# Three PSUM banks taken through one pool of three buffers, or through three names strictly in turn

## The chip, the cores and the metric

One NeuronCore of a Trainium2 chip runs the kernel. The metric is device time in microseconds (us), the median of the timed executions; in the profiles it is the span of one execution. Differences are judged from executions of both kernels on one chip, in the same rounds. Engines are named PE or TensorE (matmul), PEld (its weight loads), DVE or VectorE, ACT or ScalarE, POOL or GpSimd, SP or SyncE.

## The reference

A recurrent retention layer (4 sequences, 8 heads, 768 steps, head size 64) feeds a two-layer network with a SiLU between (3072 tokens, 512 to 2048 to 512), all in fp32:

```python
for t in range(S):                               # attention, by head with decay gamma
    state = gamma * state + einsum('bhd,bhe->bhde', k[:, :, t], v[:, :, t])
    y[:, :, t] = scale * einsum('bhd,bhde->bhe', q[:, :, t], state)
x = y.transpose(0, 2, 1, 3).reshape(B * S, H * D)
h = x @ w_in
out = (h * (1 / (1 + exp(-h)))) @ w_out
```

## The kernel before

The sequence is cut into 6 chunks of 128 steps. A *visit* handles one chunk of one sequence: TensorE transposes k and q (tiles kp and qp), forms scores and state sums, then the outputs y. A *product* is 1/16 of the first layer for one chunk: 8 matmuls into the accumulator ha and 4 into hb (three fp32 products of split operands, for accuracy). Visits are woven in between products. The results g go to memory and come back for the last stage, the second layer.

PSUM has eight banks here: two for the scores (s), two for y, one for qp (q), and three that kp, ha and hb share, through one name with three buffers. The framework picks a bank from those that are free when it lays out the program, and adds a semaphore wait to the first matmul of a tile for whoever used that bank last.

```python
ps_u = pool("ps_u", 1, space=PS)
ps_h = pool("ps_h", 3, space=PS)
...
def turn(name):
    return ps_h.tile([128, 512], FP32, tag="h", name=name)
...                                                  # in a visit
for name, to, bufs, src, tp in (
        ("kt", kt, 2, kqv["k"][n], turn(f"kp_{n}")),
        ("qt", qt, 3, kqv["q"].pop(n), banks("q", f"qp_{n}", 1)[:, 0])):
    ...                                              # 4 transposes by TensorE into tp
    evac[:] = [nc.scalar.copy(out=to[n], in_=tp).ins]          # ScalarE empties kp, qp
...
def product_in(c, f):
    ha, hb = turn(f"ha_{c}_{f}"), turn(f"hb_{c}_{f}")
    for i in range(3):
        for kk in range(KIN):
            nc.tensor.matmul(hb if i == 2 else ha, ...)
    hs = hpool.tile([128, NT], FP32, tag="hs", name=f"g_{c}_{f}")
    nc.scalar.activation(out=hs, in_=ha, func=AF.Copy, scale=ONE_E)        # empties ha
    nc.vector.tensor_tensor(out=hs, in0=hs, in1=hb, op=ALU.subtract)       # empties hb
    nc.scalar.activation(out=hs, in_=hs, func=AF.Silu)
...                                                  # last stage: accumulators of 4 sequences
acc.append([turn(f"oa{b}_{c}"), turn(f"ob{b}_{c}") if b == 2 else
            banks("q", f"ob{b}_{c}", 1)[:, 0]])
...
nc.scalar.dma_start(out=out[...], in_=o)             # outputs leave by ScalarE's queue
```

TensorE's order is the program's own; the framework orders the other engines.

Of the kernel before, what the change touches and what calls it, by code (L numbers as in the profile page):

```python
# [12 lines left out]
FP32 = mybir.dt.float32  # L13
# [18 lines left out]
def kernel(  # L32
# [42 lines left out]
    PS = bass.MemoryType.PSUM  # L75

    def pool(name, bufs, **kw):
        return ctx.enter_context(tc.tile_pool(name=name, bufs=bufs, **kw))
# [8 lines left out]
    stage = pool("stage", 2)  # L87
    conv = pool("conv", 1)
    ps_u = pool("ps_u", 1, space=PS)
    ps_h = pool("ps_h", 3, space=PS)  # L90

    g_dram = {(c, f): dram.tile([128, NT], FP32, tag=f"g{c}_{f}", name=f"gd_{c}_{f}")
              for c in range(NC) for f in range(NF)}
# [186 lines left out]
    def banks(tag, name, n=2):  # L280
        return ps_u.tile([128, n, 512], FP32, tag=tag, name=name)

    def turn(name):
        return ps_h.tile([128, 512], FP32, tag="h", name=name)

    token = const.tile([1, 1], FP32, tag="token", name="token")

# [22 lines left out]
    def stage_t(n):  # L310
# [4 lines that stand above are left out]
            tp = tp.rearrange("p (a t) -> p a t", a=HP)  # L315
            for a in range(HP):
                nc.tensor.transpose(tp[:, a, :], src[:, 2 * a : 2 * a + 2, :], ident)
            to[n] = one.tile([128, HP, C], FP32, tag=name, name=f"{name}_{n}", bufs=bufs)
            evac[:] = [nc.scalar.copy(out=to[n], in_=tp).ins]
# [148 lines left out]
# [4 lines that stand above are left out]
                nc.tensor.matmul(hb if i == 2 else ha, lhsT=w_sb[f][:, i, ts(kk, 128)],  # L472
                                 rhs=xt[c][:, i, kk, :], start=kk == 0 and i != 1,
                                 stop=kk == KIN - 1 and i != 0)
        hs = hpool.tile([128, NT], FP32, tag="hs", name=f"g_{c}_{f}")
        nc.scalar.activation(out=hs, in_=ha, func=AF.Copy, scale=ONE_E)  # L476
        nc.vector.tensor_tensor(out=hs, in0=hs, in1=hb, op=ALU.subtract)  # L477
        nc.scalar.activation(out=hs, in_=hs, func=AF.Silu)  # L478
        pending.append((c, f, hs))
# [95 lines left out]
    for c in range(NC):  # L575
        acc = []
        for b in range(B):
            if b < 2:
                u = banks("sy"[b], f"o{b}_{c}")
                acc.append([u[:, i] for i in range(2)])  # L580
            else:
                acc.append([turn(f"oa{b}_{c}"), turn(f"ob{b}_{c}") if b == 2 else
                            banks("q", f"ob{b}_{c}", 1)[:, 0]])
        for f in range(NF):
            n = c * NF + f
            split(n + S_AHEAD)
            t = ready.pop(n)
            first_, last = f == 0, f == NF - 1
            for b in range(B):
                gh, glo, gm = (t[:, i, ts(b, C)] for i in range(3))  # L590
                oa, ob = acc[b]
                nc.tensor.matmul(oa, lhsT=gh, rhs=wo[f][:, 0, :], start=first_, stop=False)  # L592
                nc.tensor.matmul(oa, lhsT=glo, rhs=wo[f][:, 1, :], start=False, stop=last)  # L593
                nc.tensor.matmul(ob, lhsT=gm, rhs=wo[f][:, 2, :], start=first_, stop=last)  # L594
        for b in range(B):
            oa, ob = acc[b]
            o = one.tile([128, DM], FP32, tag=("kt", "qt")[b % 2], name=f"o_{c}_{b}",
                         bufs=(2, 3)[b % 2])
            nc.scalar.activation(out=o, in_=oa, func=AF.Copy, scale=ONE_E)
            nc.vector.tensor_tensor(out=o, in0=o, in1=ob, op=ALU.subtract)  # L600
            nc.scalar.dma_start(out=out[ds(b * S + c * C, C), :], in_=o)
# [30 lines left out]
```

## Time and profile before

| | before |
|---|---|
| time, median of 3 executions | 658.88 us (657.73 to 659.81) |
| span of the profiled execution | 659.4 us |
| TensorE busy | 619.9 us, 94% |
| idle of TensorE up to 92 us | 24.5 us |
| waits of TensorE for one of the three banks, by the list of waits | 6.2 us |

The profile lines are shown in the prediction: busy times first, then the stretches, then TensorE's waits.

### The profile page before, as it was taken

The numbers are of one execution on the slowest core, as the hardware profiler recorded it, in microseconds if no ns is written. First come the engines' busy times: TensorE is split into PE (matmuls) and PEld (weight loads), VectorE is DVE, ScalarE is ACT, GpSimd is POOL, SyncE is SP. The second block draws the span as 40 slices with busy tenths as digits, with TensorE's granted clock in tenths as the row PEclk, the third lists the DMA queues.
The fourth block names the chain that finished last, engine by engine and source line by source line (L and its number), as shares of the span: only waits on it lengthen the run. The fifth ranks groups of instructions, "written<-read, shape, count | busy, mean of one in ns | idle before, by whom it ended". The sixth has DMA issues, their size and how long they took to land.

```text
span 659.4 us, 13529 instructions
## 1 busy us (share of the span) xinstructions
PE 619.9 (94%) x5440; PEld 507.2 (77%) x5440; DVE 429.2 (65%) x740; ACT 282.0 (43%) x510; POOL 14.2 (2%) x94
## 2 busy tenths in 40 slices
PE   3679898999999989999999999999999999999996
PEld 2557786778778877888878888888888888888885
DVE  4988887989666886775948757454463545554631
ACT  5435555757544445444548863222131412222311
POOL 2000100000000000000000000000000000000000
PEclk9869999999999999999999999999999999999999
DMA  9967777555656776766646645342343432423301
GB/s 204 205 153 172 194 185 198 171 175 187 213 153 183 207 223 181 225 178 223 196 157 198 195 147 163 89 167 93 100 156 100 133 123 95 160 95 97 129 0 64
DMA packets 123070, 103.64 MB, mean 157 GB/s; under 512 B 80000, under 2 KB 88192, under 8 KB 123008
## 3 DMA queue, kind: packets, MB, share of 16 engines
q1 hardware_dynamic: 119552, 96.49, 50.7%
q10 hardware_dynamic: 3456, 6.29, 2.6%
q8 instruction: 42, 0.69, 0.4%
q14 instruction: 20, 0.16, 0.1%
HBM read 66.06 MB, written 36.70 MB: 156 GB/s over the span
## 4 chain that ended last, share of the span: by engine, by line
PE 66%; DVE 16%; DMA 6%; ACT 5%; issue 3%; SPq 2%; POOL 0%; ACTq 0%; DVEq 0%; POOLq 0%
PE ha L472 15%; PE hb L472 8%; PE ob L594 7%; PE o L594 7%; PE o L592 7%; PE oa L592 7%; PE o L593 7%; PE oa L593 7%; DMA wf<-in_moe_w_in_dram 3%; DVE g L477 2%; DVE cs L189 2%; DVE cp L193 2%; PE y L375 2%; DVE xt L417 1%; ACT ca L182 1%
## 5 line engine op out<-in xcount | busy, mean ns | idle before, releaser
L472 PE MATMUL ha<-xt,wi 128*128 128x512 f32 x768 | 197.3, 398 | 9.9 <-DVE g L477 4.3
L472 PEld LDWEIGHTS ha<-xt,wi 128*128 128x128 f32 x768 | 142.2, 189 | 47.0 <-DVE g L477 9.0
L519 DVE TENSOR_TENSOR gs<-gr,gs 128x512 fp32r<-128x512 f32 x96 | 62.2, 686 | 89.5 <-ACT gs L517 89.5
L517 ACT ACTIVATE gs<-gr 128x512 fp32r<-128x512 f32 x96 | 53.6, 621 | 134.1 <-issue 131.8
L472 PE MATMUL hb<-xt,wi 128*128 128x512 f32 x384 | 104.4, 394 | 0.5 <-ACT g L476 0.2
L477 DVE TENSOR_TENSOR g<-g,hb 128x512 f32<-128x512 f32 x96 | 65.7, 684 | 50.4 <-PE hb L472 39.6
L478 ACT ACTIVATE g<-g 128x512 f32<-128x512 f32 x96 | 60.6, 631 | 77.0 <-DVE g L477 76.2
L472 PEld LDWEIGHTS hb<-xt,wi 128*128 128x128 f32 x384 | 72.1, 189 | 18.1 <-ACT g L476 1.5
L594 PE MATMUL ob<-wo,gs 128*128 128x512 f32 x192 | 75.2, 392 | 0.0
L592 PE MATMUL o<-wo,gs 128*128 128x512 f32 x192 | 74.7, 389 | 0.0
L592 PE MATMUL oa<-wo,gs 128*128 128x512 f32 x192 | 74.7, 389 | 0.0
L594 PE MATMUL o<-wo,gs 128*128 128x512 f32 x192 | 74.7, 389 | 0.0
L593 PE MATMUL o<-wo,gs 128*128 128x512 f32 x192 | 74.7, 389 | 0.0
L593 PE MATMUL oa<-wo,gs 128*128 128x512 f32 x192 | 74.7, 389 | 0.0
L476 ACT ACTIVATE g<-ha 128x512 f32<-128x512 f32 x96 | 56.4, 588 | 28.7 <-PE ha L472 25.6
L520 DVE SCALAR_TENSOR_TENSOR gs<-gs 128x512 fp32r<-128x512 f32 x96 | 62.0, 685 | 0.0
L594 PEld LDWEIGHTS ob<-wo,gs 128*128 128x128 f32 x192 | 36.0, 188 | 8.9 <-DVE o L600 1.6
L593 PEld LDWEIGHTS o<-wo,gs 128*128 128x128 f32 x192 | 36.0, 188 | 7.6
L594 PEld LDWEIGHTS o<-wo,gs 128*128 128x128 f32 x192 | 36.0, 188 | 7.5
L592 PEld LDWEIGHTS oa<-wo,gs 128*128 128x128 f32 x192 | 36.0, 188 | 7.5
L593 PEld LDWEIGHTS oa<-wo,gs 128*128 128x128 f32 x192 | 36.0, 188 | 7.5
L592 PEld LDWEIGHTS o<-wo,gs 128*128 128x128 f32 x192 | 36.0, 188 | 7.3
(71 smaller groups left out, 639.9 us busy)
## 6 DMA issues: line engine op xcount, KB each, us to landing
gd<-g SPq DMA_DIRECT2D x96, 256.0 KB, 3.0
gr<-gd SPq DMA_DIRECT2D x96, 256.0 KB, 2.7
wf<-in_moe_w_out_dram SPq DMA_DIRECT2D x16, 512.0 KB, 4.3
kf<-in_k_dram SPq DMA_DIRECT2D x24, 256.0 KB, 4.9
qf<-in_q_dram SPq DMA_DIRECT2D x24, 256.0 KB, 4.5
vf<-in_v_dram SPq DMA_DIRECT2D x24, 256.0 KB, 4.9
out_dram<-o ACTq DMA_DIRECT2D x24, 256.0 KB, 2.1
wf<-in_moe_w_in_dram SPq DMA_DIRECT2D x16, 256.0 KB, 3.4
```

Of the source, the lines that this page charges most:

```text
L189: nc.vector.scalar_tensor_tensor(out=s, in0=a, scalar=3, in1=s, op0=ALU.logical_shift_left, op1=ALU.bitwise_or)
L193: nc.vector.scalar_tensor_tensor(out=p.bitcast(FP32), in0=lo, scalar=2.0 ** -52, in1=p.bitcast(FP32), op0=ALU.mult, op1=ALU.mult)
L472: nc.tensor.matmul(hb if i == 2 else ha, lhsT=w_sb[f][:, i, ts(kk, 128)], rhs=xt[c][:, i, kk, :], start=kk == 0 and i != 1, stop=kk == KIN ...
L476: nc.scalar.activation(out=hs, in_=ha, func=AF.Copy, scale=ONE_E)
L477: nc.vector.tensor_tensor(out=hs, in0=hs, in1=hb, op=ALU.subtract)
L478: nc.scalar.activation(out=hs, in_=hs, func=AF.Silu)
L517: nc.scalar.activation(out=t[:, 0, :], in_=g, func=AF.Copy, scale=HALF)
L519: nc.vector.tensor_tensor(out=t[:, 1, :], in0=g, in1=high, op=ALU.subtract)
L520: nc.vector.scalar_tensor_tensor(out=t[:, 2, :], in0=t[:, 1, :].bitcast(FP32), scalar=-1.0 / EPS, in1=high, op0=ALU.mult, op1=ALU.add)
L592: nc.tensor.matmul(oa, lhsT=gh, rhs=wo[f][:, 0, :], start=first_, stop=False)
L593: nc.tensor.matmul(oa, lhsT=glo, rhs=wo[f][:, 1, :], start=False, stop=last)
L594: nc.tensor.matmul(ob, lhsT=gm, rhs=wo[f][:, 2, :], start=first_, stop=last)
```

## The change

Its intent is to take the three banks strictly in turn, each under a name of its own, rather than as the layout happens to find them free.

```diff
-    ps_h = pool("ps_h", 3, space=PS)
+    ps_h = pool("ps_h", 1, space=PS)
...
+    turns = [0]
+
     def turn(name):
-        return ps_h.tile([128, 512], FP32, tag="h", name=name)
+        turns[0] += 1
+        return ps_h.tile([128, 512], FP32, tag=f"h{turns[0] % 3}", name=name)
```

## The prediction

> **What bounds the kernel now.** I read the page first (busy times and the strip of 40 slices), then the busy times by stage, then TensorE's list of waits, and last the timeline around the place where, as will be seen, the change acts.
>
> ```profile
> PE 619.9 (94%) x5440; PEld 507.2 (77%) x5440; DVE 429.2 (65%) x740; ACT 282.0 (43%) x510; POOL 14.2 (2%) x94
> ...
> PE   3679898999999989999999999999999999999996
> ...
> PEclk9869999999999999999999999999999999999999
> ```
>
> The first line is busy time by engine, the second TensorE's share of each of 40 slices in tenths, the third its granted clock. TensorE is the bound: 619.9 of 659.4 us, and only the first three slices, of 16.5 us each, are below 8 tenths.
>
> ```profile
> core 0: us, PE busy (x) PEld busy (x) DVE busy (x) ACT busy (x) POOL busy (x), PEclk, DMA share, GB/s
> 0.00:92.00 92.00, 67.53 (x1408) 55.43 (x1408) 72.77 (x135) 45.38 (x93) 8.48 (x62) 0.91 0.81 185
> 92.00:192.00 100.00, 95.15 (x718) 75.51 (x711) 80.56 (x142) 60.22 (x105) 1.49 (x6) 1.00 0.60 185
> 192.00:391.00 199.00, 194.13 (x2172) 159.85 (x2171) 141.78 (x246) 106.68 (x188) 4.21 (x26) 1.00 0.65 194
> 391.00:659.40 268.40, 263.13 (x1157) 216.41 (x1155) 134.10 (x217) 69.72 (x126) 0.00 (x0) 1.00 0.34 110
> ```
>
> This is busy time by stretch. From 92 us on TensorE is busy 95.15 of 100, 194.13 of 199 and 263.13 of 268.40 us. The only stretch with room is the first, with 92 - 67.53 = 24.5 us idle, and it is also where attention fills the state and the first products start. What TensorE waits for:
>
> ```profile
> PE kp L317 <- DMA kf<-in_k_dram: 10.3, 2, 7.0
> PE y L375 <- DVE xt L417: 8.5, 4, 3.3
> PE ha L472 <- DVE g L477: 4.3, 9, 1.6
> PE ha L472 <- DVE xt L417: 3.4, 3, 1.4
> PE kp L317 <- DVE g L477: 1.7, 3, 1.4
> ...
> PE hb L472 <- ACT g L476: 0.2, 1, 0.2
> ```
>
> The columns are total us, times, longest us. The three banks that the change is about hold kp (k's transposes), ha and hb (the two halves of a product). A wait for one of these banks can only show as a wait for whoever empties it: ScalarE's copy of kp (line 319), ScalarE's reading of ha (line 476), VectorE's subtraction that reads hb (line 477). Such rows sum to 4.3 + 1.7 + 0.2 = 6.2 us, 0.94% of the span. That is a ceiling: even a perfect handling of these banks could not give 2% (13.2 us). The larger rows wait for an input's transfer or for the split of x, which the change doesn't touch.
>
> **What the Trainium skill says.** "Perfetto Trace Analysis", section "Matmuls", says independent groups of matmuls should rotate through different PSUM banks, so that emptying one overlaps the matmuls of the next. The kernel before does so already, and the trace agrees: at 63.37 us TensorE writes the next ha while ScalarE reads the last one from 63.87 and VectorE the last hb from 65.68. "PSUM — Partial Sum Buffer", section "The four PSUM rules", says that each bank is a separate SRAM and one matmul targets a single bank. Nothing there makes one bank slower than another. The trace shows no difference either: all 768 matmuls into ha have a median of 389 ns and all 384 into hb too, over all three banks. "Perfetto Trace Analysis", section "Identifying Dependency Chains", says to look at the semaphores that an instruction waits for. That settles this case, since a bank's name costs nothing by itself: only a different wait can.
>
> **The change part by part.** It removes no instruction and adds none. It replaces one pool name with three buffers by three names with one buffer each, the name chosen by a counter. So it can act in only two ways: another order of instructions, or another bank, and with it another wait, for some tile. I built both kernels and compared them. The order on all five engines is the same, row for row. TensorE's order is fixed by the program anyway.
>
> Of the tiles that go through the turn (24 kp, 192 ha and hb, and 18 accumulators of the last stage, three for each of six chunks) eight get another bank. With the three banks called 5, 6, 7:
>
> ```
> tile:    kp0 kp1 kp2 kp3 kp4 kp5 ha0 hb0 kp6 ha1 hb1 kp7 ha2 hb2 ha3 hb3 kp8
> before:   5   7   6   5   7   6   5   7   6   5   7   6   5   6   7   5   6
> after:    5   6   7   5   6   7   5   6   7   5   6   7   5   6   7   5   6
> ```
>
> (ha0 is the first product of chunk 0, and so on.) The pool of three was therefore already taken in turn everywhere, but with 6 and 7 exchanged at first; at hb2 the two swapped once, and from there on before and after are the same bank for bank to the end. While the labels are merely exchanged, each tile follows the same predecessor in its bank, so its wait is the same. Only the two tiles at the swap have another predecessor, and the built programs differ in exactly two waits, both on TensorE: hb2 waited for ScalarE's copy of kp7, and will wait for VectorE's subtraction that reads hb1; ha3 has it the other way round. All other semaphore waits, over all engines, have the same semaphore and value.
>
> Are these two on the path? The timeline of before, TensorE, then VectorE, then ScalarE:
>
> ```profile
> 55.15 1.08 PE L472 MATMUL hb<-xt,wi 128*128 128x512 f32 x4
> 56.07 0.60 PE L317 MATMUL kp<-ident,kf 128*128 128x128 f32 x4
> ...
> 62.46 1.07 PE L472 MATMUL hb<-xt,wi 128*128 128x512 f32 x4
> 63.37 1.98 PE L472 MATMUL ha<-xt,wi 128*128 128x512 f32 x8
> ```
>
> ```profile
> 58.30 0.68 DVE L477 TENSOR_TENSOR g<-g,hb 128x512 f32<-128x512 f32 x1
> ```
>
> ```profile
> 56.76 0.58 ACT L319 COPY kt<-kp 128x512 f32<-128x512 f32 x1 [0.81 <-PE kp L317]
> ```
>
> The columns are start, duration, engine. These are hb1, kp7, hb2, ha3, and the two that empty hb1 and kp7. (I counted forward from the first product, at 42 us: ha0, hb0, kp6, ha1, hb1, kp7, ha2, hb2, ha3.) The subtraction ends at 58.30 + 0.68 = 58.98, the copy at 56.76 + 0.58 = 57.34. The weight loads of hb2 and ha3 start at 62.23 and 63.14 in TensorE's timeline, a little before their matmuls. So:
> - hb2: its new wait is over 62.23 - 58.98 = 3.25 us before it is needed (the old one 4.89 us before).
> - ha3: its new wait is over 63.14 - 57.34 = 5.80 us before (the old one 4.16 us).
>
> TensorE waits for neither before nor after. What holds it there is its own order, the attention matmuls and ha2 ahead of hb2. Cost of the parts: instructions 0, order 0, six relabelled tiles ahead of the swap with the same neighbours 0, the other two relabelled ones (hb1, kp7) 0 in themselves, two waits 0. The sum is 0.0 us.
>
> **The rivals.** (1) *The strict turn makes a tile wait for a bank while another is free.* A pool gives any free bank, a named one only itself. For it: the 1.7 us of kp behind the subtraction is just such a wait. Against: the two programs have the same predecessor there, so those 1.7 us exist already and remain. If the margin at hb2 were gone, the worst would be that hb2's four matmuls (0.91 us, from 62.46 to 63.37) no longer ran ahead of the subtraction: at most 0.9 us, 0.14%, about 660. It would take a VectorE 3.25 us late there. (2) *The strict turn gains*, by removing the 6.2 us of bank waits: 652.7, by the row sums. Against: all those waits stand unchanged in the built program. (3) *Bank 6 and 7 exchanged changes something in the memory itself*, for instance beside the neighbouring banks of the scores and of q. Nothing in the trace speaks for it, and no two engines share a bank that did not before. It would touch eight tiles in the first 60 us: tenths of a microsecond at most, my guess. (4) *The state of the chip or run to run spread* is the one thing that will show: the three runs of before are 657.73, 658.88 and 659.81.
>
> **Range and chances.** The prediction is the median of before, 658.9. The three runs have a standard deviation of about 1.0 us; a median of three then has some 0.7, and the difference of two such medians 0.7 x 1.41 = 1.0, of which 1.28 is 1.3 us for 8 in 10. I widen it to 1.8 for another hour or chip: 657.1 to 660.7. A change of over 2% needs 13.2 us, twice the ceiling of the gain and over ten times the worst loss worked out above; I leave 1% on each side for a disturbed run.
>
> **What would show it right or wrong.** Right: the same number of instructions on each engine; the rows of bank waits (4.3, 1.7, 0.2) within some tenths; no idle time ahead of hb2 and ha3 at about 62 us; busy time from 92 us on unchanged; time inside the spread of before. Wrong: a row "hb waits for the subtraction" in TensorE's waits, an idle gap before hb2, matmuls of the eight tiles longer than the same ones before (those up to 50 us run at a lower clock in both), or a stage after 92 us that is longer with the same instructions, which would mean that something other than waits depends on the names.

## More of the kernel before

A matmul of 512 columns is shown with 389 ns, but in an unbroken row the next one starts 227 ns after it, since they are pipelined. So idle time *between shown bars* is less than the delay of the next start, by up to 389 - 227 = 162 ns for every gap.

## The result, and the profile after

| | before | after |
|---|---|---|
| time, median of 4 executions each | 658.99 us (657.73 to 659.81) | 659.43 us (658.01 to 660.24) |
| ratio, with its 95% interval | | 1.0006 (0.9982 to 1.0030) |

A ratio is the mean time of one kernel's fast executions over that of the other's in the same rounds, so not quite the ratio of the two medians. The change did nothing that can be measured.

The page of the kernel after, its busy times, TensorE's strip and the granted clock:

```profile
PE 619.6 (94%) x5440; PEld 507.6 (77%) x5440; DVE 429.1 (65%) x740; ACT 282.4 (43%) x510; POOL 14.2 (2%) x94
...
PE   3679898999999989999999999999999999999996
...
PEclk9869999999999999999999999999999999999999
```

The instruction counts are the same, and the strips of TensorE and of the clock are the same digit for digit. Busy time by stretch, kernel after (columns as in the prediction; the last stretch ends with the span, at 658.5 us):

```profile
0.00:92.00 92.00, 67.88 (x1432) 55.83 (x1436) 72.77 (x135) 45.74 (x94) 8.50 (x62) 0.91 0.80 185
92.00:192.00 100.00, 95.19 (x702) 75.76 (x694) 80.51 (x142) 59.91 (x104) 1.48 (x6) 1.00 0.60 186
192.00:391.00 199.00, 194.24 (x2173) 160.15 (x2172) 141.69 (x246) 107.59 (x188) 4.20 (x26) 1.00 0.63 194
391.00:658.50 267.50, 262.26 (x1154) 215.86 (x1152) 134.11 (x217) 69.13 (x126) 0.00 (x0) 1.00 0.32 110
```

In the first three stretches TensorE's busy time moves by at most 0.4 us and ScalarE's by at most 0.9 us; the last stretch is cut 0.9 us shorter because the span is. TensorE's waits, kernel after (total us, times, longest):

```profile
PE kp L320 <- DMA kf<-in_k_dram: 9.9, 3, 6.6
PE y L378 <- DVE xt L420: 8.6, 4, 3.4
PE ha L475 <- DVE g L480: 3.9, 7, 1.6
...
PE kp L320 <- DVE g L480: 2.0, 3, 1.4
...
PE hb L475 <- ACT g L479: 0.2, 1, 0.2
```

The rows of waits for a bank come to 3.9 + 2.0 + 0.2 = 6.1 us, where before had 6.2. There is no new row of hb waiting for the subtraction. And the place of the change, in the timeline of the kernel after, TensorE, VectorE, ScalarE:

```profile
54.47 1.07 PE L475 MATMUL hb<-xt,wi 128*128 128x512 f32 x4
55.38 0.60 PE L320 MATMUL kp<-ident,kf 128*128 128x128 f32 x4
...
61.52 1.08 PE L475 MATMUL hb<-xt,wi 128*128 128x512 f32 x4
62.44 1.98 PE L475 MATMUL ha<-xt,wi 128*128 128x512 f32 x8
```

```profile
57.66 0.68 DVE L480 TENSOR_TENSOR g<-g,hb 128x512 f32<-128x512 f32 x1
```

```profile
56.07 0.58 ACT L322 COPY kt<-kp 128x512 f32<-128x512 f32 x1 [0.80 <-PE kp L320]
```

The weight loads of hb2 and ha3, with which their waits end, in the kernel before and then in the kernel after:

```profile
62.23 0.87 PEld L472 LDWEIGHTS hb<-xt,wi 128*128 128x128 f32 x4
63.14 1.77 PEld L472 LDWEIGHTS ha<-xt,wi 128*128 128x128 f32 x8
```

```profile
61.30 0.88 PEld L475 LDWEIGHTS hb<-xt,wi 128*128 128x128 f32 x4
62.22 1.77 PEld L475 LDWEIGHTS ha<-xt,wi 128*128 128x128 f32 x8
```

The subtraction that hb2 now waits for ends at 57.66 + 0.68 = 58.34, and hb2's weights are loaded at 61.30, 2.96 us later. The copy that ha3 now waits for ends at 56.07 + 0.58 = 56.65, and ha3's weights are loaded at 62.22, 5.57 us later. TensorE shows no gap before either.

### The profile page after: what moved, and what is told of

It reads as the page before. It is cut to its first block, busy times and chain, and to the rows that moved or that the text cites. A ratio compares the mean times of both kernels' runs of the same rounds, so it can differ in the third digit from the quotient of the medians.

```text
span 658.5 us, 13529 instructions
## 1 busy us (share of the span) xinstructions
PE 619.6 (94%) x5440; PEld 507.6 (77%) x5440; DVE 429.1 (65%) x740; ACT 282.4 (43%) x510; POOL 14.2 (2%) x94
## 4 chain that ended last, share of the span: by engine, by line
PE 71%; DVE 14%; DMA 6%; ACT 5%; issue 3%; SPq 1%; POOL 0%; ACTq 0%; DVEq 0%; POOLq 0%
PE ha L475 18%; PE hb L475 9%; PE ob L597 7%; PE o L597 7%; PE o L596 7%; PE oa L596 7%; PE o L595 7%; PE oa L595 7%; DMA wf<-in_moe_w_in_dram 2%; DVE g L480 2%; PE y L378 2%; DVE cs L189 2%; DVE cp L193 2%; PE kp L320 1%; ACT ca L182 1%
## 5 line engine op out<-in xcount | busy, mean ns | idle before, releaser
L597 PEld LDWEIGHTS ob<-wo,gs 128*128 128x128 f32 x192 | 36.1, 188 | 8.8 <-DVE o L603 1.6
L596 PEld LDWEIGHTS o<-wo,gs 128*128 128x128 f32 x192 | 36.1, 188 | 7.5
L597 PEld LDWEIGHTS o<-wo,gs 128*128 128x128 f32 x192 | 36.1, 188 | 7.5
L596 PEld LDWEIGHTS oa<-wo,gs 128*128 128x128 f32 x192 | 36.1, 188 | 7.5
L595 PEld LDWEIGHTS o<-wo,gs 128*128 128x128 f32 x192 | 36.1, 188 | 7.3
```

The costliest lines, as they stand in the source:

```text
L595: nc.tensor.matmul(oa, lhsT=gh, rhs=wo[f][:, 0, :], start=first_, stop=False)
L596: nc.tensor.matmul(oa, lhsT=glo, rhs=wo[f][:, 1, :], start=False, stop=last)
L597: nc.tensor.matmul(ob, lhsT=gm, rhs=wo[f][:, 2, :], start=first_, stop=last)
```

## The experiments

A null result is easily right for the wrong reason, so the runs ask four things. How small a difference can be seen at all? Does a bank, or the act of taking it in turn, cost anything by itself? Do bank waits cost time in this kernel when they are late? And what are the 6.2 us of bank waits worth that the change left in place?

| run | what | ratio to before | 95% interval |
|---|---|---|---|
| e1_aa, e10_aa2 | before against itself | 0.9998, 1.0001 | 0.9980 to 1.0015, 0.9981 to 1.0021 |
| e2_again | the change again | 0.9994 | 0.9975 to 1.0014 |
| e3_moved | all PSUM tiles in other banks | 0.9998 | 0.9980 to 1.0016 |
| e4_swap, e8_swap2 | the swap at 38 places | 0.9978, 0.9990 | 0.9960 to 0.9996, 0.9965 to 1.0016 |
| e7_late | one late wait at the same place | 1.0024 | 1.0005 to 1.0042 |
| e6_two | one bank each for ha, hb, kp | 1.0266 | 1.0249 to 1.0283 |
| e5_four, e9_four2 | turn of four banks | 0.9913, 0.9922 | 0.9898 to 0.9928, 0.9901 to 0.9944 |
| e11_four_sp | turn of four, outputs by SyncE | 0.9877 | 0.9858 to 0.9896 |
| e12_three_sp | turn of three, outputs by SyncE | 0.9986 | 0.9966 to 1.0007 |

All twelve gave correct results. The edits are to the changed kernel unless said otherwise.

**The resolution, and the change again.** e1_aa is the kernel before, unchanged.

> The kernel before, unchanged, run against itself. Every theory expects a ratio of 1.000; what the interval leaves open is the resolution of the other runs. Expected half-width of the interval 0.2 to 0.3%.

> The changed kernel again, with more rounds than the first time. Theory (only two waits differ, both long satisfied): ratio 1.000, within the same interval as the run of before against itself, that is within 0.998 and 1.002. Rival 1 (the strict turn costs a wait): up to +0.9 us, 1.001. Rival 2 (the strict turn gains the bank waits): down to -6.2 us, 0.991.

Before against itself gives 0.9998, with half an interval of 0.18%, or 1.2 us. The change again gives 0.9994. The worst case of rival 1 (0.9 us) is smaller than what these rounds can resolve, so the time alone doesn't exclude it; the trace does, with the same three rows of bank waits (3.9, 1.7 and 0.5 us) and no hb behind the subtraction. Rival 2 (0.991) is excluded.

**Other banks, same waits.** The two PSUM pools are opened in the other order.

```diff
-    ps_u = pool("ps_u", 1, space=PS)
     ps_h = pool("ps_h", 1, space=PS)
+    ps_u = pool("ps_u", 1, space=PS)
```

> The changed kernel with the pool of the three banks opened ahead of the other PSUM pool, so that all tiles of products and transposes, and those of scores, outputs and q too, lie in other physical banks; every instruction and every wait is the same as in the changed kernel. Theory (a bank costs nothing by itself): ratio 1.000, within 0.998 and 1.002. Rival 3 (which bank matters in itself): a difference that grows with the tiles moved, all of them in place of 8; if 8 tiles were worth tenths of a us, some 230 are worth several us, over 0.5%.

The built program has every instruction and wait of the changed kernel. The ratio is 0.9998. Which bank a tile lies in has no cost that these runs can see (they resolve some 1.3 us), and rival 3 is out at any size that matters here.

**The swap, 38 times.** Where a kp lies between two products, the next hb takes kp's bank and a later tile that of the earlier hb.

```diff
-    turns = [0]
+    turns, free, seen = [0], [1, 2, 0], []
...
+        if name.startswith("hb") and seen[-2:-1] == ["kp"]:
+            free[0], free[1] = free[1], free[0]
+        seen.append(name[:2])
+        free.append(free.pop(0))
-        return ps_h.tile([128, 512], FP32, tag=f"h{turns[0] % 3}", name=name)
+        return ps_h.tile([128, 512], FP32, tag=f"h{free[-1]}", name=name)
```

> The swap that the pool of three made once is made after every transpose of k among the products: there the next hb takes the bank of kp and a later tile that of the hb before. 38 waits of TensorE differ from the changed kernel, with the same order on all engines. From the traces of before and after, the new bank of each of these 38 tiles was empty at least 3.3 us before its weight load. Theory (only waits that end last cost): ratio 1.000, within 0.998 and 1.002; the rows of bank waits unchanged at some 4, 2 and 0.2 us. Rival 1 (taking banks out of turn, or in turn, is worth something in itself): 19 times what one swap is worth, either sign.

The first ratio, 0.9978, had an interval just below 1, against my expectation. Rather than explain it I ran the same kernel again, beside another run of before against itself:

> The kernel of the 38 swaps again, unchanged, since its first ratio was 0.9978 with an interval from 0.9960 to 0.9996, where the theory had 1.000. If that was chance (its profile shows the same rows of bank waits as before, and all of its 1 us lead arises between 42 and 79 us, in the stretch where the granted clock changes): a ratio between 0.998 and 1.002 now. If the swap itself is worth something: 0.998 again or lower.

> The kernel before against itself again, beside the two repeats: ratio 1.000, interval half-width 0.2%.

The second ratio is 0.9990, its interval holds 1, and before against itself gave 1.0001. So no effect of a size that matters is shown. In both profiles of the swap, though, the stretch from the first to the seventh product is 36.1 and 36.4 us long, against 36.9 to 37.5 in the seven profiles of turns of three without the swap or a late wait (before three times, after twice, all banks moved, outputs by SyncE). That is some 0.9 us by the means, 0.1%. Only 4 of the 19 swaps (38 waits) lie in that stretch. From the seventh product to the end, with the other 15, both profiles of the swap take 580 us, and so do the seven others (579.2 to 580.5). So the lead doesn't grow with the number of swaps, though rival 1 of the expectation had every swap worth the same. Whether the swap causes it, and how, stays open.

**One late wait at the very place.** hb2 doesn't advance the turn, and so takes the bank of ha2.

```diff
-        turns[0] += 1
+        if name != "hb_0_2":
+            turns[0] += 1
```

> One wait made late on purpose at the very place of the change: hb2 takes the bank of ha2, just ahead of it, the turn goes on from there in the same way. In the trace of before ScalarE's reading of ha2 ends 2.2 us after hb2's weights are loaded. Theory (the two changed waits cost nothing because they are early, not because waits there are free): a wait of about 2.3 us shows ahead of hb2, and the first stage ends later by 1 to 2.5 us, ratio 1.001 to 1.004, at the edge of what the rounds resolve; the trace decides. Rival (any wait at this place is hidden by later slack): the idle time shows, but the time from 92 us on is the same.

TensorE's timeline in this run:

```profile
59.83 2.11 PE L476 MATMUL ha<-xt,wi 128*128 128x512 f32 x8
64.49 1.49 PE L476 MATMUL hb<-xt,wi 128*128 128x512 f32 x4 [2.55 <-ACT g L480]
65.77 3.32 PE L476 MATMUL ha<-xt,wi 128*128 128x512 f32 x8
```

The bracket is the idle time ahead and what ended it: 2.55 us for ScalarE's reading of ha2. The seventh product starts at 81.79 us, where after had 78.94 and before 79.31, and the kernel ends at 661.0, where after had 658.5 and before 659.4. The ratio is 1.0024, some 1.6 us (the interval allows 0.3 to 2.8), so more than half of this one wait seems to have reached the end. In the built program ha3 and hb3 also have other predecessors, long done, and three neighbouring instructions each of VectorE and ScalarE changed places, so the number is not purely that of the wait. What it shows is enough: a late wait at this place is not hidden; in the change it cost nothing because it was about 3 us early.

**A shallower turn.** Every ha in one bank, every hb in a second, every kp in the third.

```diff
-        turns[0] += 1
-        return ps_h.tile([128, 512], FP32, tag=f"h{turns[0] % 3}", name=name)
+        kind = {"ha": 0, "hb": 1, "kp": 2, "oa2": 0, "ob2": 1, "oa3": 2}
+        bank = next(b for n, b in kind.items() if name.startswith(n))
+        return ps_h.tile([128, 512], FP32, tag=f"h{bank}", name=name)
```

> The turn is cut down: every ha in one bank, every hb in a second, every kp in the third. Theory (names matter only through who had the bank before): ha then follows the ha before it, and in the trace of before 75 of 95 would be needed before the old one is read, hb in 43 to 45 of 95; the shortfalls sum to 90 us, an upper bound, since a late tile makes all that follows late and need not be paid twice; slower by 10 to 60 us, ratio 1.015 to 1.09, with long rows of ha behind ScalarE's reading of ha and hb behind the subtraction. Rival (ScalarE and VectorE set the pace of the product stages anyway, so the depth of the turn is of no account): within 1%.

TensorE's waits in this run:

```profile
PE hb L474 <- DVE g L479: 11.7, 11, 1.8
...
PE ha L474 <- ACT g L478: 6.3, 5, 1.6
```

The kernel is 2.7% slower (676.74 us against 659.1), in the expected range but at its lower end; the 90 us of shortfalls were an upper bound, as expected. The rows of bank waits are 11.7 + 6.3 = 18.0 us, where after had 6.1. This run doesn't change the waits alone: in the built program the framework also put some instructions of VectorE, ScalarE and SyncE in another order, so a part of the 2.7% may be that. It is small: late starts behind a bank, counted as in the section on why the prediction was right, are 22.3 us here and 8.7 in before, which makes 13.6 of the 14.4 us by which the products took longer. The names matter as soon as they give a tile a later predecessor.

**A deeper turn.** The bank of q's transposes stands idle whenever there is no visit. It joins the turn.

```diff
-        return ps_h.tile([128, 512], FP32, tag=f"h{turns[0] % 3}", name=name)
+        return ps_h.tile([128, 512], FP32, tag=f"h{turns[0] % 4}", name=name)
...
-                ("qt", qt, 3, kqv["q"].pop(n), banks("q", f"qp_{n}", 1)[:, 0])):
+                ("qt", qt, 3, kqv["q"].pop(n), turn(f"qp_{n}"))):
...
-                acc.append([turn(f"oa{b}_{c}"), turn(f"ob{b}_{c}") if b == 2 else
-                            banks("q", f"ob{b}_{c}", 1)[:, 0]])
+                acc.append([turn(f"oa{b}_{c}"), turn(f"ob{b}_{c}")])
```

> The bank of q's transposes joins the turn: four banks strictly in turn for kp, qp, ha, hb, and for the last stage's accumulators. Same order on all engines; 184 waits of TensorE differ. From the trace of before, with a turn of four every bank would be empty at least 0.44 us before it is needed (24 of 213 handovers have no margin now). Theory (bank waits are worth just what the rows of waits show, and the change left them all in place): the rows ha and kp behind the subtraction (4.3 and 1.7 us) and hb behind ScalarE (0.2) go, and the time falls by 2 to 6 us, ratio 0.991 to 0.997. Rival (these waits only stand in front of other waits, for the split of x or for transfers, that take their place): rows gone, time the same, 0.999 to 1.001.

TensorE's waits in this run:

```profile
PE ha L475 <- DVE xt L420: 4.4, 3, 2.1
PE oa L594 <- ACT o L601: 2.6, 2, 1.4
...
PE qp L320 <- DVE g L480: 0.9, 1, 0.9
...
PE hb L475 <- DVE g L480: 0.3, 1, 0.3
```

The rows of ha and kp behind the subtraction are gone; 0.9 and 0.3 us are left for qp and hb, though by the trace of before every bank was to be empty 0.44 us early. The ratio is 0.9913 (653.1 us against 659.1). By the trace the products (from the first ha to the first matmul of the last stage) took 340.8 us, against 349.5 before (349.2 to 349.7 in the five profiles of before and after): 8.7 us less, more than the 6.2 us of the rows. The last stage took 270.8 us against 267.4: 3.4 us were given back. Its new row, an accumulator waiting for ScalarE, leads to ScalarE's timeline in this run:

```profile
469.26 3.24 ACTq L603 DMA_DIRECT2D out_dram<-o  x3
472.55 0.60 ACT L601 ACTIVATE o<-oa 128x512 f32<-128x512 f32 x1 [2.87 <-DMA out_dram<-o]
```

Three issues of outputs' transfers on ScalarE's queue took from 469.26 to 472.50; the same three took 1.61 us before. One of them lasted 1.96 us in place of 0.34, and only then could ScalarE read the accumulator that TensorE wanted next.

> The turn of four again, unchanged. Its first profile had the product stage 8.6 us shorter and the last stage 2.9 us longer, because two of the 24 issues of an output's transfer on ScalarE's queue took 2.0 us in place of 0.34 us and held up ScalarE's reading of an accumulator. If these two are part of the new arrangement: again some issues over 1 us in the last stage, and a ratio of 0.991. If they were chance: none, a span of some 650.5 us in the profile, and among the timed runs again some near 652.5 and some near 655.

Again two long issues, the third output of the second and of the fourth chunk as the first time (1.4 and 1.9 us), again a longer last stage (270.1 us), and 340.1 us of products; ratio 0.9922. So it isn't chance, and the part of the gain that was given back is named. The remedy to try is to issue these transfers from SyncE, which does nothing else here than issue transfers:

```diff
-            nc.scalar.dma_start(out=out[ds(b * S + c * C, C), :], in_=o)
+            nc.sync.dma_start(out=out[ds(b * S + c * C, C), :], in_=o)
```

> The turn of four, and the transfers of the outputs issued from SyncE's queue in place of ScalarE's. In both profiles of the turn of four two of these issues held ScalarE up (for 2.0 and 2.1, then 1.4 and 1.9 us), and the last stage was 3.4 and 2.7 us longer than the 267.4 us of before. If the late reading of the accumulator behind those issues is what was given back: no wait of an accumulator for ScalarE, last stage 267.5 us again, time 648 to 651 us, ratio 0.984 to 0.988. If the stall comes from the transfers themselves (queue or memory) and holds up something on SyncE's queue in the same way: last stage as long as with the turn of four, ratio 0.991 to 0.992.

> The control of that run: the changed kernel (turn of three) with the outputs' transfers issued from SyncE's queue. No issue took over 0.38 us in any profile of a turn of three, so there is nothing to win: ratio 1.000, within 0.997 and 1.002, if the queue itself costs nothing; over 1.002 if issuing from SyncE puts outputs behind waiting loads.

The ratio is 0.9877 (651.31 us against 659.52), the fastest version found, 1.2% below before. The issues of the outputs in this run, now on SyncE's queue:

```profile
L603 SPq DMA_DIRECT2D out_dram<-o x24: 332/337/1425, 427.3 to 646.8; - x24
```

The three numbers are shortest, median and longest in ns. The long issues are still there: 1.43 us at the third output of the second chunk, and 1.35 us at the fourth of the fourth chunk. But no wait of an accumulator is left in TensorE's list, and the last stage took 266.0 us. So the stall goes with the transfers, not with ScalarE; what causes it is not settled. In all three profiles it came at 470 to 472 us and at 558 to 560 us from the start, when the turns of three issue no outputs. Nor does it belong to the turn of four: in nine of the ten profiles of a turn of three, one or two loads of g on SyncE's queue took 0.8 to 1.4 us to issue in the last stage, in place of 0.32, at 417 to 419, 505 to 507 or 593 to 595 us (1.04 us at 505.74 in the trace of before). They too lie some 88 us, two chunks of the last stage, apart. There the last stage took 267.4 to 267.5 us with such an issue or without (265.9 in e12_three_sp); in the turn of four the stall fell on an output, ahead of ScalarE's next reading. The products took 342.0 us, 1 to 2 us more than in the other two profiles of the turn of four, which I leave unexplained; in e12_three_sp they took 350.8, 1.1 to 1.5 us more than before and after. With a turn of three (e12_three_sp), where no output's issue was long, the last stage took 265.9 us too, 1.5 us less than before, but the ratio, 0.9986, has an interval that holds 1. Of the 4.1 to 4.8 us by which SyncE's queue shortened the last stage of the turn of four, then, 1.5 us may be this and not the stall.

## Why the prediction was right

- **The two waits.** The prediction read margins of 3.25 and 5.80 us from the trace of before; the trace after has 2.96 and 5.57. e7_late shows that a late wait at the same tile does cost (1.0024), so the margins are the reason, and not some slack further on.
- **Six relabelled tiles and the other two, at 0.** Confirmed well beyond eight tiles: all of them moved gave 0.9998. The prediction's own evidence was weaker than it reads: a median of 389 ns over all three banks can't tell one bank from another. Taken bank by bank in the same trace, it is 389 ns for ha and for hb in each of the three.
- **Its example of overlap** holds for ScalarE, which reads ha at 63.87 us while the next ha is written (63.37 to 65.35). VectorE's subtraction at 65.68 comes after that; it overlaps the next hb, written from 65.18. Nothing rests on it.
- **Rival 1, the strict turn makes a tile wait.** Its mechanism is real: e6_two, which gives tiles worse predecessors, loses 2.7%. It didn't act because the pool of three had taken the banks in the same turn all along, but for one swap.
- **Rival 2 and its ceiling of 6.2 us.** The mechanism was right, and nothing of it happened. The size was too small. The prediction called the sum of the rows of bank waits a ceiling; taking those waits away with a fourth bank shortened the products by 8.7 us. Part of the term that was missed is the reading of idle time. In the trace of before I looked at the 24 tiles of the product stage whose weight load starts within 150 ns of their bank being emptied, and summed how much later than normal their first matmul starts (over 227 ns after a 512-column matmul, over 60 ns after a smaller one): 8.7 us, where the idle between bars gives 6.2. After has 8.9 for 22 such tiles, so the change removed none of it. The turn of four has 15 and 2.0 us left, a fall of 6.7 us; the remaining 2 us or so of its gain I haven't traced. 8.7 us is still less than the 13.2 that 2% needs.
- **The range.** 659.43 lies inside 657.1 to 660.7, and 0.5 us from the value named. Single executions of before scattered over 657.48 to 661.54, but its medians lay between 658.88 and 659.59 in all rounds, so the unwidened 1.3 us would have held too: the widening was not put to the test. A miss of 0.5 us is within the scatter and says no more than that.

## What to carry to other kernels

A change of buffers' names is judged by asking, for each tile, who had the buffer before and how long that user had been done: where the predecessor was the same or its margin positive, the change was worth nothing here, however different the source looks. The list of waits of the engine that sets the pace shows what a better arrangement could gain, though starts of matmuls give the size more truly than idle time between their bars. And a bank that idles through a stage, lent to the turn of another, was worth more here than any order within the turn that was tried, until the engine that empties it was held up by its own queue.

## What the Trainium skill lacked or had wrong

- "Perfetto Trace Analysis", section "Tensor Engine Instruction (MATMUL, LD_WEIGHTS)", says that a matmul's end is estimated from its size. It warns against matmul busy time as a measure, but doesn't draw the consequence for idle time: here bars of 389 ns at starts 227 ns apart hid up to 162 ns of every gap, so 8.7 us of late starts read as 6.2 us of idle.
- The same page, section "Matmuls", advises rotating through banks, and another section using all eight, but neither says what a bank more or less is worth. Here, over 96 products with visits between, one bank each for ha, hb and kp cost 2.7%, and a fourth bank in the turn of three gained 0.8 to 0.9%.
- "PSUM — Partial Sum Buffer" doesn't say whether banks are alike in speed. All tiles moved to other banks gave 0.9998 (0.9980 to 1.0016).
- "Perfetto Trace Analysis", section "DMA Instruction — HWDGE (DVE, Sync)", lists what the issue of a transfer consists of, but no page that was searched says when one takes several times as long. Here two outputs of 24 took 1.4 to 2.1 us to issue, in place of 0.34, in each of three profiles of the turn of four, and one or two loads of g took 0.8 to 1.4 us, in place of 0.32, in nine of ten profiles of a turn of three. On ScalarE's queue they held up its next read; on SyncE's they cost nothing that shows.
